# Evacuating the turned attention probabilities of the first batch straight from PSUM into their high and low halves

## The chip, the cores and the metric

The kernel runs on one core of one Trainium2 chip. The metric is device time in microseconds (us) for one launch; the lower the better. The core has five engines with instruction queues of their own: PE (TensorE, matrix products), DVE (VectorE), ACT (ScalarE), POOL (GpSimd) and SP (SyncE, which here only issues DMAs). SBUF is the on-chip memory of 128 partitions; PSUM is the accumulator memory of eight banks, into which PE writes.

## The reference

Cut to what matters, for `q`, `k`, `v` of shape (8 batches, 8 heads, 576 tokens, 64):

```python
k_p = k.reshape(B, H, Sp, 8, D).mean(axis=3)         # keys and values pooled by 8: Sp = 72
v_p = v.reshape(B, H, Sp, 8, D).mean(axis=3)
s = scale * q @ k_p^T
p = exp(s - max(s)); p = p / (sum(p) + 1e-9)
x = (p @ v_p), transposed to (4608 tokens, 512)
x = ((x @ w1) * (x @ w2)) @ w3 @ w_out               # 512 -> 1024 -> 1024 -> 512
h = x @ w_in                                         # 512 -> 2048
out = (h * sigmoid(1.702 * h)) @ w_out2              # 2048 -> 512
```

The weights arrive as 64-bit floats; the kernel turns them into 32-bit ones itself.

## The kernel before, in words

All large products are made at nearly the accuracy of 32-bit floats out of a faster format (called fp32r in the profile). Each operand is split into a high half (the value rounded to that format) and a low half (the value minus the high half), and a product is three matmuls: high by high, high by low, low by high (`mm3`, L114 to L116; `mm3u`, L709, in the last stage). A split is one copy on ACT (`split`, L104) and one subtraction on DVE or POOL (L105).

The work has three stages.

1. A first stage, some 130 us long. The weights `w_out`, `w3`, `w1`, `w2` are loaded and converted, tile by tile, by `Conv.step` (two activations on ACT, L166 and L168; a shift on DVE, L169; an addition on POOL, L172), then split. `w3` is also turned on PE (L508) and multiplied with `w_out` (`w3_mm`, which goes through `mm3` into two accumulators). Between these steps, `tick` calls `tick_first`, which takes the first batch's attention forward: four groups (n = 0 to 3, `NPE` = 4), each of two heads.
2. The products with `w1` and `w2` and the folded `w3 w_out`, block by block of 512 tokens, with the attention of the other seven batches (groups 4 to 31) between them, in the same `tick`.
3. The last expert layer, whose weights stream from DRAM.

The attention of a group goes through these functions: `g0` turns k and q (L255, L256) and sums k by eight; `g1` makes the scores on PE (L277) into two PSUM banks and subtracts the row maximum (L282, L284); `g2` is the exponential (L293); `g3` normalizes (L300 to L303); `g4` makes the turned probabilities and their halves; `g_va` and `g_vb` pool the values and split them into `vm` and `vt` (POOL, L324 to L342; ACT, L338 to L341); `g6` multiplies (L380 to L383) into the group's two banks and splits the result into the block's `x` (L390, L391). For groups 0 to 3 the turn is made on PE against an identity matrix; the others turn with DVE (L314).

In `g4` of a group n < 4 the two banks that held the scores take the transposes: the first bank four of 128 columns (L351), the second one of 64 (L354) and three of 32 partitions (L356), and, once the first bank is read out, the last two of 32 partitions go there (L360, L361). ACT copies them out to the SBUF tiles `p0` (128 partitions, L352, L358) and `p1` (32 partitions, L359, L362). Then come the halves: `ph` holds high and low of `p0`, by an ACT copy (L368) and a POOL subtraction (L369), each of 576 columns; `pt` holds high, high again and low of `p1` in partitions 0 to 31, 32 to 63 and 64 to 95, by two ACT copies (L370, L371) and a POOL subtraction (L372). All four tiles exist once each (one buffer), in every group. Even groups of the first four use the banks `wk[2:]`, odd ones `acc[2:]`. The profile calls `p0` and `p1` together `p`, and a few tiles by the name of the slot that they lie in (`s`).

The order in which an engine gets its instructions isn't just that of the program: the context is opened with `schedule_with_timeline_sim=True`, and a planner with costs of its own places each engine's instructions, keeping the dependences, among them that a tile with one buffer isn't written again before its readers of the last group are done. In the order of the program, `tick_first` runs `g6(n)` at tick 2n + 6, ahead of `g4(n + 1)` in the same tick:

```python
for n in range(NPE):
    if t == 2 * n + 6:
        g6(n)
...
    elif s == 4:          # s = t - 2 * n
        g4(n)
        g_va(n)
    elif s == 5:
        g_vb(n)
```

SP issues the loads of weights (L151), of k and q (L229, four transfers of 72 KB each) and of v (L249, L250) in one queue.

Of the kernel before, what the change touches and what calls it, by code (L numbers as in the profile page):

```python
# [8 lines left out]
F32R = mybir.dt.float32r  # L9
# [3 lines left out]
ALU = mybir.AluOpType  # L13
# [4 lines left out]
P = 128  # L18
T = 512
# [3 lines left out]
def pooled_attention_moe_moe2(  # L23
# [18 lines left out]
    nc = tc.nc  # L42
    B, H, S, D = q.shape
# [12 lines left out]
    NPE = HP  # L56
# [34 lines left out]
    def take_a(i, dtype=F32R):  # L91

        return slota_p.tile([P, 2, T], dtype, name=f"s{i}", tag=f"s{i}")
# [6 lines left out]
    def f32(ap):  # L100
        return ap.bitcast(F32)
# [22 lines left out]
    def sl(i, n=P):  # L124
        return slice(i * n, (i + 1) * n)
# [65 lines left out]
    with pa_ctx:  # L191
        pa = pa_ctx.enter_context(tc.tile_pool(name="pa", bufs=1))
# [6 lines left out]
            out=mask[:, 0], in_=mask[:, 0], compare_op=ALU.is_gt, fill=0.0,  # L199
            base=SK, pattern=[[0, D]], channel_multiplier=-1)  # L200
        nc.gpsimd.affine_select(
            out=mask[:, 1], in_=mask[:, 1], compare_op=ALU.is_ge, fill=0.0,
# [8 lines left out]
        for t in s_ts:  # L211
# [6 lines left out]
            out=ident, in_=ident, compare_op=ALU.is_equal, fill=0.0,  # L218
# [6 lines left out]
        g_q, g_k, g_v, g_s = {}, {}, {}, {}  # L225
# [38 lines left out]
        def banks_of(n):  # L264
            return acc[2:] if n < NPE and n % 2 else wk[2:]

        def s_of(n):
            return s_ts[n % 2 if n < NPE else 0]
# [26 lines left out]
        def g3(n):  # L295
            s_t = s_of(n)
            r = banks_of(n)[0][:, T - 2 * TT:]
            pv = s_t[:, :, :KW].rearrange("p t (a s) -> p t a s", s=SK)
            rv = r.rearrange("p (t a) -> p t a", a=2)
            nc.vector.tensor_reduce(out=rv, in_=pv, op=ALU.add, axis=AX.X)  # L300
            nc.vector.tensor_scalar_add(r, r, 1e-9)
            nc.vector.reciprocal(out=r, in_=r)
            nc.vector.tensor_tensor(  # L303
                out=pv, in0=rv.unsqueeze(3).to_broadcast([P, TT, 2, SK]), in1=pv, op=ALU.mult)
            p0 = pa.tile([P, TT, P], F32, name="p0", tag="p0")
            p1 = pa.tile([32, TT, P], F32, name="p1", tag="p1")
            g_s[n] = (p0, p1)
            if n < NPE:
                return
            for r in range(5):  # L310
                for c in range(4):
                    nt = TT if 32 * (c + 1) <= S - (TT - 1) * P else TT - 1
                    dst = p0[32 * r:32 * r + 32] if r < 4 else p1[:32]
                    nc.vector.transpose(  # L314
                        out=dst[:, :nt, 32 * c:32 * c + 32],
                        in_=s_t[32 * c:32 * c + 32, :nt, 32 * r:32 * r + 32])
# [26 lines left out]
                out=vt[32:64, D:], in0=vtf, in1=f32(vt[:32, D:]), op=ALU.subtract)  # L343

        def g4(n):
            p0, p1 = g_s.pop(n)
            if n < NPE:
                ps, s_t = banks_of(n), s_of(n)
                p0f, p1f = (t.rearrange("p t c -> p (t c)") for t in (p0, p1))
                for tt in range(4):  # L350
                    nc.tensor.transpose(ps[0][:, sl(tt)], s_t[:, tt, :P], ident)  # L351
                nc.scalar.copy(p0f[:, :T], ps[0])  # L352
                w = S - T
                nc.tensor.transpose(ps[1][:, :w], s_t[:w, 4, :P], ident[:w, :w])  # L354
                for tt in range(3):
                    nc.tensor.transpose(  # L356
                        ps[1][:32, w + tt * P:w + (tt + 1) * P], s_t[:, tt, P:], ident)
                nc.scalar.copy(p0f[:, T:S], ps[1][:, :w])  # L358
                nc.scalar.copy(p1f[:, :3 * P], ps[1][:32, w:w + 3 * P])  # L359
                nc.tensor.transpose(ps[0][:32, :P], s_t[:, 3, P:], ident)  # L360
                nc.tensor.transpose(ps[0][:32, P:P + w], s_t[:w, 4, P:], ident[:w, :w])  # L361
                nc.scalar.copy(p1f[:, 3 * P:S], ps[0][:32, :P + w])  # L362
            ph = pa.tile([P, 2, S], F32R, name="ph", tag="ph")
            pt = pa.tile([96, S], F32R, name="pt", tag="pt")
            g_s[n] = (ph, pt)
            s0 = p0.rearrange("p t c -> p (t c)")[:, :S]
            s1 = p1.rearrange("p t c -> p (t c)")[:, :S]
            nc.scalar.copy(ph[:, 0], s0)  # L368
            nc.gpsimd.tensor_tensor(out=ph[:, 1], in0=s0, in1=f32(ph[:, 0]), op=ALU.subtract)  # L369
            nc.scalar.copy(pt[:32], s1)  # L370
            nc.scalar.copy(pt[32:64], s1)  # L371
            nc.gpsimd.tensor_tensor(out=pt[64:96], in0=s1, in1=f32(pt[:32]), op=ALU.subtract)  # L372
# [32 lines left out]
        def tick_first():  # L405

            t = tick_n[0]
            tick_n[0] += 1
# [4 lines that stand above are left out]
                s = t - 2 * n  # L413
                if s == 0 and n == 0:
                    g0(0)
                elif s == 1:
                    g1(n)
                elif s == 2:
                    g2(n)
                    g0(n + 1)  # L420
                elif s == 3:
                    g3(n)
                elif s == 4:
# [4 lines that stand above are left out]
            if t == 2 * NPE + 4:  # L428
                tick_n[0] = 4 * NPE
                give(s_sl)  # L430

        def tick():
            t = tick_n[0]
            if t < 4 * NPE:
                return tick_first()
            tick_n[0] += 1
            n, s = divmod(t, 4)
            if s == 0:
                if NPE <= n - 1 < NG:
                    g4(n - 1)  # L440
            elif s == 1:
                if n < NG:
                    g1(n)
            elif s == 2:
                if NPE <= n - 1 < NG:
                    g6(n - 1)
                if n < NG:
                    g2(n)
                    g_va(n)
                if n + 1 < NG:  # L450
                    g0(n + 1)
            elif n < NG:
                g3(n)
                g_vb(n)
# [147 lines left out]
        for blk in range(NB):  # L602
            x = [x_slot(blk, c) for c in range(KM)]
            if blk == NB - 2:

                pa_ctx.close()
                pa = pa_ctx.enter_context(tc.tile_pool(name="pc", bufs=1, reuse_waits="tile"))
# [10 lines left out]
            for f in range(NF1):  # L618
# [6 lines left out]
                if blk == NB - 1:  # L625
                    give(w1_s.pop(f))
                    give(w2_s.pop(f))
                    if 0 <= f - FA < KM:

                        t = take_a(f - FA)  # L630
# [41 lines left out]
    with tc.tile_pool(name="pb", bufs=1, reuse_waits="tile") as pb, \  # L672
# [206 lines left out]
        for k, f in enumerate(FO):  # L879
            bk = bank()  # L880
            w = ready.pop(("h", 0, f))
# [29 lines left out]
        for pr in range(1, NPAIR + 1):  # L911
# [17 lines left out]
            for fp in range(NFP):  # L929
# [4 lines left out]
                for name, i in ORDER:  # L934
# [6 lines left out]
                    if name in PART:  # L941
                        s, h = PART[name]
                        w = ready[s, pr, 2 * fp + i][:, h]
                    else:
                        w = ready[name, pr, fp][:, i]
# [53 lines left out]
            src = {"M5": 0, "M7": 1, "M3": 2, "M2": 3, "M4": 3, "M6": 4}  # L999
# [12 lines left out]
            m1, U, V, n = [], [], [], 0  # L1012
# [116 lines left out]
```

## Time and profile before

| | us |
|---|---|
| median of 3 runs | 1477.42 |
| lowest and highest of them | 1476.0, 1481.82 |
| the profiled execution, its own time | 1479.71 |
| span of its profile | 1478.0 |
| PE busy in the span | 1438.7 |

The span is the time between the first and the last instruction in the profile; the profiled execution's own time holds 1.71 us around it. An engine's busy time counts its instructions alone. "Idle before" an instruction, in brackets at the end of a timeline row, is the time for which its engine did nothing ahead of it, and behind the arrow stands what ended that time.

### The profile page before, as it was taken

The page shows a single profiled execution, that of the slowest core. Times are in us where ns is not written, and L with a number is a line of the kernel's source. Part 1 is how long each engine was busy: PE and PEld are TensorE (multiplying, and loading weights), DVE is VectorE, ACT ScalarE, POOL GpSimd, SP SyncE. Part 2 cuts the span into 40 slices and gives each one's busy share as a digit, 9 for nine tenths or more (in the row PEclk, how much of TensorE's full clock was granted, in tenths as well). Part 3 has the DMA queues.
Part 4 walks back from the last instruction along what each step waited for, and adds up shares of the span by engine and source line. Part 5 has one row for each costly group of instructions (what it writes and reads, how often), then busy time and mean ns, then how long its engine had stood idle before and what let it go on. Part 6 is the DMA issues. An engine that isn't in the chain of part 4 may idle for free.

```text
span 1478.0 us, 19436 instructions
## 1 busy us (share of the span) xinstructions
PE 1438.7 (97%) x6536; PEld 1190.0 (81%) x6536; DVE 988.7 (67%) x1728; ACT 693.9 (47%) x1212; POOL 489.0 (33%) x589
## 2 busy tenths in 40 slices
PE   6979999999999999999999999999999999999998
PEld 4867888888888888888788887888788888888886
DVE  7888998878787877654737255683559354944554
ACT  7875444434343433366635344552455244534442
POOL 8789656554545555366733100000000000000000
PEclk9989999999999999999999999999999999999999
DMA  9992233323232311199879978877677766785665
GB/s 265 248 233 48 57 85 57 80 46 78 49 77 49 77 33 37 42 325 344 309 236 398 325 243 276 294 211 221 194 244 224 221 197 221 239 234 180 194 213 139
DMA packets 294436, 267.64 MB, mean 181 GB/s; under 512 B 201664, under 2 KB 226240, under 8 KB 294336
## 3 DMA queue, kind: packets, MB, share of 16 engines
q1 hardware_dynamic: 291648, 265.09, 59.8%
q10 hardware_dynamic: 2688, 1.31, 0.3%
q8 instruction: 52, 0.85, 0.2%
q14 instruction: 48, 0.39, 0.1%
HBM read 209.72 MB, written 56.62 MB: 180 GB/s over the span
## 4 chain that ended last, share of the span: by engine, by line
PE 82%; DMA 7%; DVE 5%; ACT 2%; SPq 2%; issue 1%; POOL 1%; DVEq 0%; ACTq 0%; POOLq 0%
PE bk L709 39%; PE wk L114 8%; PE wk L115 8%; PE wk L116 8%; PE acc L114 4%; PE acc L115 4%; PE acc L116 4%; PE wk L277 2%; DMA wud<-wt 2%; DVE p L314 1%; SPq L229 1%; DMA st<-wind 1%; PE bk L115 1%; PE bk L116 1%; PE bk L114 1%
## 5 line engine op out<-in xcount | busy, mean ns | idle before, releaser
L709 PE MATMUL bk<-mv,st 128*128 128x512 f32 x1152 | 272.6, 391 | 0.7 <-DMA st<-wud 0.7
L709 PE MATMUL bk<-xM,st 128*128 128x512 f32 x1092 | 259.0, 390 | 3.9 <-DMA st<-wind 3.7
L709 PEld LDWEIGHTS bk<-mv,st 128*128 128x128 f32 x1152 | 217.3, 189 | 46.3 <-issue 1.1
L709 PEld LDWEIGHTS bk<-xM,st 128*128 128x128 f32 x1092 | 204.5, 188 | 48.6 <-issue 2.5
L114 PE MATMUL wk<-s,s 128*128 128x512 f32 x576 | 227.0, 396 | 2.8 <-DVE a L641 1.2
L116 PE MATMUL wk<-s,s 128*128 128x512 f32 x576 | 224.9, 391 | 2.1 <-DVE s L105 2.1
L115 PE MATMUL wk<-s,s 128*128 128x512 f32 x576 | 224.9, 391 | 0.0
L314 DVE STREAM_TRANSPOSE p<-s_t 32x160 f32<-32x160 f32 (+1 forms) x560 | 178.5, 319 | 10.3
L114 PE MATMUL acc<-s,s 128*128 128x512 f32 x352 | 134.8, 406 | 8.2 <-ACT s L104 3.2
L115 PE MATMUL acc<-s,s 128*128 128x512 f32 x352 | 141.4, 402 | 0.9 <-POOL s L105 0.8
L116 PE MATMUL acc<-s,s 128*128 128x512 f32 x352 | 140.4, 399 | 0.0
L114 PEld LDWEIGHTS wk<-s,s 128*128 128x128 f32 x576 | 108.5, 189 | 26.2 <-DVE a L641 2.1
L116 PEld LDWEIGHTS wk<-s,s 128*128 128x128 f32 x576 | 108.3, 188 | 24.8 <-DVE s L105 2.3
L115 PEld LDWEIGHTS wk<-s,s 128*128 128x128 f32 x576 | 108.4, 188 | 22.1 <-DVE s L391 0.4
L105 DVE TENSOR_TENSOR mv<-g,mv 128x1024 fp32r<-128x1024 f32 x80 | 97.8, 1222 | 33.6 <-ACT mv L104 32.2
L104 ACT CAST mv<-g 128x1024 fp32r<-128x1024 f32 x80 | 84.3, 1054 | 71.8 <-PE bk L709 71.4
L172 POOL TENSOR_TENSOR cv<-cv,s 128x512 int32<-128x512 int32 x72 | 97.5, 1364 | 28.6 <-DVE cv L169 21.1
L105 POOL TENSOR_TENSOR s<-a,s 128x512 fp32r<-128x512 f32 x56 | 72.5, 1294 | 82.5 <-ACT s L104 62.7
L638 ACT COPY a<-wk 128x512 f32<-128x512 f32 x72 | 42.1, 585 | 110.5 <-PE wk L116 89.7
L369 POOL TENSOR_TENSOR ph<-p,ph 128x576 fp32r<-128x576 f32 x32 | 45.7, 1429 | 126.5 <-ACT ph L368 123.9
L114 PEld LDWEIGHTS acc<-s,s 128*128 128x128 f32 x352 | 67.8, 193 | 23.4 <-ACT s L104 5.2
L115 PEld LDWEIGHTS acc<-s,s 128*128 128x128 f32 x352 | 68.2, 194 | 15.0 <-POOL s L105 2.0
(190 smaller groups left out, 2357.9 us busy)
## 6 DMA issues: line engine op xcount, KB each, us to landing
st<-wud SPq DMA_DIRECT2D x96, 512.0 KB, 4.4
st<-wind SPq DMA_DIRECT2D x66, 512.0 KB, 4.7
st<-wind SPq DMA_DIRECT2D x76, 256.0 KB, 3.9
s<-in_moe_w_dram SPq DMA_DIRECT2D x32, 512.0 KB, 6.4
wind<-s SPq DMA_DIRECT2D x32, 512.0 KB, 5.4
s<-in_moe_w_out_dram SPq DMA_DIRECT2D x24, 512.0 KB, 6.5
kr<-in_k_dram SPq DMA_DIRECT2D x128, 72.0 KB, 2.6
qr<-in_q_dram SPq DMA_DIRECT2D x128, 72.0 KB, 2.6
```

The source lines that it names most:

```text
L104: nc.scalar.copy(dst[:, 0], src)
L105: lo_eng.tensor_tensor(out=dst[:, 1], in0=src, in1=f32(dst[:, 0]), op=ALU.subtract)
L114: nc.tensor.matmul(o, a[:, 0, a_sl], b[:, 0, b_sl], start=first, stop=False)
L115: nc.tensor.matmul(o, a[:, 0, a_sl], b[:, 1, b_sl], start=False, stop=False)
L116: nc.tensor.matmul(o, a[:, 1, a_sl], b[:, 0, b_sl], start=False, stop=last)
L172: nc.gpsimd.tensor_tensor(out=w.bitcast(I32), in0=w.bitcast(I32), in1=lo_w.bitcast(I32), op=ALU.add)
L229: nc.sync.dma_start(dst[32 * c:32 * c + 32], src[b, 2 * hp + c // 2, :, 32 * (c % 2):32 * (c % 2) + 32].rearrange("(g t) d -> t g d", t=32))
L277: nc.tensor.matmul(sc[half][:, i * KW:(i + 1) * KW], qT[:, sl(tt)], mov, start=True, stop=True)
L314: nc.vector.transpose(out=dst[:, :nt, 32 * c:32 * c + 32], in_=s_t[32 * c:32 * c + 32, :nt, 32 * r:32 * r + 32])
L369: nc.gpsimd.tensor_tensor(out=ph[:, 1], in0=s0, in1=f32(ph[:, 0]), op=ALU.subtract)
L638: nc.scalar.copy(a, pa_)
L709: nc.tensor.matmul(o, w[:, x, m], b[:, y], start=first and n == 0, stop=last and n == 2, skip_group_check=True)
```

## The change

For groups 0 to 3, `g4` no longer copies the transposes to `p0` and `p1`. ACT copies each piece of a bank straight to the high half in `ph` (512 and 64 columns) or `pt` (384 and 192 columns), DVE subtracts that from the same piece in PSUM to give the low half, and for `pt` ACT copies the piece from PSUM a second time, to the second high half. POOL has no part in it any more. `ph` and `pt` are taken at the head of `g4`; `p0` and `p1` are no longer taken in `g3` for these groups. Groups 4 to 31 are as before.

```diff
@@ g3 @@
+            if n < NPE:
+                return
             p0 = pa.tile([P, TT, P], F32, name="p0", tag="p0")
             p1 = pa.tile([32, TT, P], F32, name="p1", tag="p1")
             g_s[n] = (p0, p1)
-            if n < NPE:
-                return
@@ g4 @@
-            p0, p1 = g_s.pop(n)
+            ph = pa.tile([P, 2, S], F32R, name="ph", tag="ph")
+            pt = pa.tile([96, S], F32R, name="pt", tag="pt")
             if n < NPE:
                 ps, s_t = banks_of(n), s_of(n)
-                p0f, p1f = (t.rearrange("p t c -> p (t c)") for t in (p0, p1))
+                w = S - T
+
+                def main(c, src):
+                    nc.scalar.copy(ph[:, 0, c], src)
+                    nc.vector.tensor_tensor(
+                        out=ph[:, 1, c], in0=src, in1=f32(ph[:, 0, c]), op=ALU.subtract)
+
+                def tail(c, src):
+                    nc.scalar.copy(pt[:32, c], src)
+                    nc.vector.tensor_tensor(
+                        out=pt[64:96, c], in0=src, in1=f32(pt[:32, c]), op=ALU.subtract)
+                    nc.scalar.copy(pt[32:64, c], src)
+
                 for tt in range(4):
                     nc.tensor.transpose(ps[0][:, sl(tt)], s_t[:, tt, :P], ident)
-                nc.scalar.copy(p0f[:, :T], ps[0])
-                w = S - T
+                main(slice(0, T), ps[0])
                 nc.tensor.transpose(ps[1][:, :w], s_t[:w, 4, :P], ident[:w, :w])
                 for tt in range(3):
                     nc.tensor.transpose(
                         ps[1][:32, w + tt * P:w + (tt + 1) * P], s_t[:, tt, P:], ident)
-                nc.scalar.copy(p0f[:, T:S], ps[1][:, :w])
-                nc.scalar.copy(p1f[:, :3 * P], ps[1][:32, w:w + 3 * P])
+                main(slice(T, S), ps[1][:, :w])
+                tail(slice(0, 3 * P), ps[1][:32, w:w + 3 * P])
                 nc.tensor.transpose(ps[0][:32, :P], s_t[:, 3, P:], ident)
                 nc.tensor.transpose(ps[0][:32, P:P + w], s_t[:w, 4, P:], ident[:w, :w])
-                nc.scalar.copy(p1f[:, 3 * P:S], ps[0][:32, :P + w])
-            ph = pa.tile([P, 2, S], F32R, name="ph", tag="ph")
-            pt = pa.tile([96, S], F32R, name="pt", tag="pt")
+                tail(slice(3 * P, S), ps[0][:32, :P + w])
+                g_s[n] = (ph, pt)
+                return
+            p0, p1 = g_s.pop(n)
             g_s[n] = (ph, pt)
```

## Rows read from the trace of the kernel before

**Rows 1.** Windows of the whole span: us, busy us of each engine, PE clock, DMA share, GB/s

```profile
0.00:130.00 130.00, 104.86 (x475) 81.50 (x476) 107.12 (x175) 100.91 (x207) 106.00 (x121) 0.93 0.87 218
250.00:640.00 390.00, 390.00 (x1873) 329.80 (x1872) 304.12 (x736) 158.01 (x353) 200.10 (x276) 1.00 0.28 66
700.00:1478.00 778.00, 765.04 (x3354) 629.30 (x3352) 441.37 (x520) 348.28 (x475) 64.27 (x48) 1.00 0.74 239
```

**Rows 2.** Windows of ten us, from group 1's `g4` to group 4's turn

```profile
60.00:70.00 10.00, 10.00 (x53) 7.85 (x52) 7.66 (x16) 9.84 (x25) 5.94 (x7) 1.00 0.91 218
70.00:80.00 10.00, 7.05 (x44) 5.49 (x41) 6.85 (x12) 7.37 (x17) 6.93 (x9) 1.00 1.01 224
80.00:90.00 10.00, 8.53 (x34) 6.98 (x35) 8.92 (x15) 8.28 (x19) 9.69 (x12) 0.83 1.07 212
90.00:100.00 10.00, 8.64 (x35) 6.53 (x34) 6.46 (x10) 8.32 (x18) 7.94 (x10) 0.83 0.98 231
100.00:110.00 10.00, 7.54 (x37) 5.84 (x36) 9.83 (x12) 6.86 (x16) 9.40 (x12) 0.93 1.19 249
110.00:120.00 10.00, 9.72 (x44) 7.95 (x43) 9.92 (x22) 7.52 (x15) 9.63 (x10) 0.90 0.36 67
```

**Rows 3.** Timeline of PE: start, us, what [idle before <-releaser]

```profile
75.70 0.40 PE L380 MATMUL acc<-ph,vm 128*128 128x288 f32 x1 [0.61 <-DVE s L284]
81.47 0.76 PE L114 MATMUL acc<-s,s 128*128 128x512 f32 x1 [2.84 <-ACT ph L368]
94.02 0.50 PE L114 MATMUL acc<-s,s 128*128 128x512 f32 x1 [1.36 <-DVE s L105]
104.73 0.54 PE L382 MATMUL acc<-ph,vm 128*128 128x288 f32 x2 [0.39 <-POOL vm L339]
107.79 0.50 PE L116 MATMUL wk<-s,s 128*128 128x512 f32 x1 [2.06 <-DVE s L105]
```

**Rows 4.** Tiles `ph`, `pt`, `p`, first 112 us: count, ns shortest/median/longest, first and last start

```profile
L368 ACT CAST ph<-p x4: 655/668/677, 36.9 to 93.3; 128x576 fp32r<-128x576 f32 x4
L369 POOL TENSOR_TENSOR ph<-p,ph x4: 1412/1429/1612, 38.4 to 95.5; 128x576 fp32r<-128x576 f32 x4
L370 ACT CAST pt<-p x4: 655/660/667, 40.7 to 94.6; 32x576 fp32r<-32x576 f32 x4
L372 POOL TENSOR_TENSOR pt<-p,pt x4: 1420/1429/1487, 41.8 to 99.1; 32x576 fp32r<-32x576 f32 x4
L359 ACT COPY p<-wk x2: 463/464/466, 36.5 to 70.9; 32x384 f32<-32x384 f32 x2
L362 ACT COPY p<-wk x2: 293/302/311, 38.7 to 75.8; 32x192 f32<-32x192 f32 x2
```

**Rows 5.** Line 105 on DVE from PSUM, first 130 us

```profile
L105 DVE TENSOR_TENSOR s<-wk,s x16: 675/690/692, 10.7 to 85.7; 128x512 fp32r<-128x512 f32 x16
```

**Rows 6.** Timeline of DVE, a subtraction of 64 columns

```profile
65.17 0.21 DVE L391 TENSOR_TENSOR s<-wk,s 128x64 fp32r<-128x64 f32 x1
```

**Rows 7.** Line 169 on DVE, first 130 us

```profile
L169 DVE TENSOR_SCALAR cv<-cv x39: 385/911/3137, 5.3 to 129.2; 128x512 uint32<-128x512 uint32 x39
```

**Rows 8.** Timelines of DVE (first row) and POOL around group 3

```profile
101.82 3.14 DVE L169 TENSOR_SCALAR cv<-cv 128x512 uint32<-128x512 uint32 x1
99.12 1.43 POOL L372 TENSOR_TENSOR pt<-p,pt 32x576 fp32r<-32x576 f32 x1
102.98 1.28 POOL L105 TENSOR_TENSOR s<-cv,s 128x512 fp32r<-128x512 f32 x1
104.23 0.45 POOL L339 TENSOR_TENSOR vm<-vf,vm 128x128 fp32r<-128x128 f32 x1
```

**Rows 9.** Timeline of ACT around group 2's `g4`, and line 390 later

```profile
68.56 0.59 ACT L352 COPY p<-wk 128x512 f32<-128x512 f32 x1
80.79 0.68 ACT L368 CAST ph<-p 128x576 fp32r<-128x576 f32 x1
111.55 0.21 ACT L390 CAST s<-acc 128x64 fp32r<-128x64 f32 x1 [0.19 <-DVE s L391]
```

## The prediction

> **What bounds the kernel now.** I read the windows of the whole span first, because the change touches four groups of a kernel with 32. The reader should compare PE's busy time with the length of each window. From 250 to 640 us PE is busy all of 390.00 us, from 700 to the end 765.04 of 778 [rows 1]. There the kernel is bound by PE, and nothing that ACT, DVE or POOL gain would show. In the first 130 us PE is busy 104.86 us only, at a granted clock of 0.93, while DVE, ACT and POOL are each busy 101 to 107 us and the DMA share is 0.87 [rows 1]. So this stage is bound by no single engine: four of them and the loads hand on to each other. A microsecond that PE gains in it comes out at the end, since PE is full afterwards; one that PE doesn't see is worth nothing.
>
> The change acts from group 0's `g4` (its first copy to `ph` starts at 36.9 us [rows 4]) to group 3's product. The windows of ten us show where PE has anything to win: it is full from 60 to 70, and from 70 to 120 it is idle 2.95, 1.47, 1.36, 2.46 and 0.28 us, 8.5 in all [rows 2]. The clock means of 0.83, 0.83, 0.93 and 0.90 in the four windows from 80 on cost another 1.7 + 1.7 + 0.7 + 1.0 = 5.1 us of full-speed work [rows 2]. Together 13.6 us is the most that the stretch can give back. That estimate ends at 120 us, where the change no longer acts.
>
> Then the timeline of PE, for what ended each idle time. The largest were ended by VectorE's splits or by what stands beside them: 2.84 us at 81.47, 1.36 at 94.02, 2.06 at 107.79; one of 0.39 at 104.73 by POOL's low half of the values [rows 3]. None of the five waits for a low half of `ph` or `pt`. What the change takes away is thus not itself on PE's path, and can help only through the queues that it stood in.
>
> **What goes.** POOL loses two subtractions per group, 1.43 us each [rows 4]: 2.86 us, 11.4 us in four groups. ACT loses three copies of 576 columns at 0.66 to 0.67 us, 2.00 us together, of which two rows stand [rows 4].
>
> **What comes.** ACT gets the two short copies to `pt` a second time, 0.464 + 0.302 us [rows 4]. Its four copies out of PSUM stay and only change their target. Net, ACT loses 2.00 - 0.77 = 1.23 us per group, 4.9 in all. DVE gets four subtractions per group with one side in PSUM. The one of 512 columns costs 0.69 us [rows 5], the one of 64 0.21 [rows 6]; on the line between these two, 0.55 for 384 and 0.35 for 192 columns (ACT's copies of 32 partitions take the time that their columns call for, so I don't expect fewer partitions to be cheaper or dearer). That is 1.80 us per group, 7.2 in all. PE's transposes and products stay as they are, and no DMA is added or removed.
>
> **Where it lies on the path.** First, POOL. Group 3's subtraction to `pt` ends at 100.55, and POOL then has a backlog: line 105 at 102.98 and the values' low half at 104.23 [rows 8]. PE waits 0.39 us for the latter [rows 3]. With 2.86 us of work gone ahead of it, this wait goes: 0.39 us. In the same place VectorE's shift (L169) takes 3.14 us [rows 8], where the shortest takes 0.385 and the median 0.911 [rows 7]; it began at 101.82 and ended with POOL's run of work. The VectorE split behind it is what PE waits 2.06 us for at 107.79 [rows 3]. If the shift is held by one POOL instruction of 1.28 us [rows 8] in place of several, it ends 3.14 - 1.28 = 1.86 us earlier. I take 1.86 (bounds: nothing, if other POOL work slides into the same place, and 2.75, if the shift takes 0.385).
>
> The page "SBUF — State Buffer" of the Trainium skill (section "Who interferes with whom") says that VectorE, in some instructions, and GpSimd lock a shared port pair for a whole instruction. By that rule up to 11.4 us of VectorE waiting could go with POOL's 11.4 us, instead of the 1.86 taken here; the shift of 3.14 us agrees with the rule, but the sum goes by the row.
>
> Of the clock's loss after these gaps, 0.7 us from 100 to 110 and 1.0 from 110 to 120 [rows 2], I count half as regained, 0.85 us (bounds nothing and 1.7). ACT was busy 9.84 of 10 us from 60 to 70 [rows 2], so 1.23 us less there may let the loads behind it start sooner. Against this stand waits of ACT, below, 3 x 0.19 = 0.57 us per group; of the 0.66 us that is left I count half, 0.33, because the DMA share is at 0.91 to 1.19 up to 110 us [rows 2] and an earlier issue finds busy DMA engines. Gains: 0.39 + 1.86 + 0.85 + 0.33 = 3.4 us.
>
> **The waits that come.** ACT's copies and VectorE's subtractions now read the same PSUM bank in turn. In the trace line 390's copy of 64 columns waits 0.19 us for VectorE's subtraction of other columns in the same bank [rows 9]. So three copies per group (`pt`'s first in the second bank and the second high half twice) wait for VectorE, and everything queued on ACT behind them waits too: conversions (L166, L168) and splits (L104). Price: 0.19 us each by that row, up to 3.14 us when a shift is stuck ahead [rows 8].
>
> The page "PSUM — Partial Sum Buffer" (section "PSUM bank collisions raise a hardware error") of the Trainium skill has this as a rule: two engines may not access the same bank and quadrant at one time, reads included. The row of 0.19 us shows the wait that keeps to it.
>
> VectorE's added 1.80 us mostly finds room: it is idle 2.3, 3.2, 1.1 and 3.5 us in the windows from 60 to 100 [rows 2]. The exception is group 3. Its three short subtractions, 1.11 us, fall just before the split that PE waits for at 94.02 [rows 3]. I count half, 0.6 us (bounds 0 and 1.1).
>
> Third, `ph` has one buffer. Until now the first copy of group 2 went to `p0` at 68.56, and only the copy to `ph` at 80.79 had to let group 1's product read the old halves [rows 9]; that product began at 75.70 [rows 3]. Now the first copy has to wait for it, until about 77.0 (eight matmuls), 8.4 us later than before. PE's last two transposes need that bank read out by ACT and then VectorE, 0.59 + 0.69 us more: 78.3. PE is in order, and what is queued behind them waits. Before, PE sat idle 2.84 us up to 81.47 anyway [rows 3], which hides the wait if the planner puts the transposes there; put right behind the product they hold PE for 1.3 us. I take 0.7.
>
> **Sum.** 3.4 - 0.6 - 0.7 = 2.1 us less. The profiled execution's own 1479.71 us (span 1478.0 and 1.71 around it) would become 1477.6. It lay 2.3 us above the median, 1477.42; off the median the forecast is 1475.3. Half a per cent, about what a measurement of this kernel can tell from no change, is 7.4 us: below 1470.0 is faster, above 1484.8 slower.
>
> **Rivals.**
> *The loads bound the stretch.* Then ACT's and POOL's relief ends in waiting for weights and keys: 1477.4. For it: the DMA share near 1 up to 110 us [rows 2]. Against: the waits of PE at 94.02 and 107.79 were ended by VectorE, not a load [rows 3].
> *POOL's relief cascades.* If VectorE's shifts are held less all along, two thirds of the 13.6 us come back: 9.0 us, 1468.4. For it: the shift's median of 0.911 against 0.385 [rows 7], over 39 shifts 20 us. Against: POOL's own 106 us [rows 1] fall only by a ninth.
> *ACT waits for VectorE, and the time grows.* Twelve copies wait in one bank for a subtraction that itself may stand behind a held shift. At 0.19 + 0.911 = 1.10 us each that is 13.2 us, less the 4.9 saved: 8.3 us, and 1485.7 if all of it reaches PE. It decides from (7.4 + 4.9) / 12 = 1.0 us per wait. For it: ACT is full from 60 to 70. Against: it has 2.6, 1.7 and 1.7 us idle in the next three windows [rows 2], and the planner may put other work ahead of a copy that waits.
>
> **Chances and range.** Forecast 0.50, loads 0.28, cascade 0.12, ACT's waits 0.10. The planner may also change the order on every engine, which the rows can't price; it widens each case by about 3 us. Faster by over 0.5%: the cascade and a tail of the forecast, 0.14. Slower: ACT's waits, 0.10. Within: 0.76. The range of 1468 to 1484 leaves out about half of the cascade, most of ACT's waits and a little of the rest, 2 in 10 together.
>
> **What the profile after would show.** No subtraction to `ph` or `pt` on POOL before 110 us; four more on DVE per group at 0.69, 0.55, 0.35 and 0.21 us, hardly varying; a shorter shift near 101; the gap at 107.79 gone; group 2's first copy behind group 1's product. PE's busy time after 130 us should not change. The prediction is wrong if ACT's idle time before lines of `g4` grows to several us and PE's idle with it, or if PE's gaps from 70 to 120 nearly vanish.

## The result, and the profile after

The changed kernel takes 1486.44 us in the median of six runs (1484.08 to 1490.33), the kernel before, run beside it, 1479.12 us (1476.0 to 1481.82). The ratio is 1.0051, with a 95% interval of 1.0035 to 1.0066: about 7.5 us slower. The forecast was 1475.3 us in a range of 1468 to 1484, so the time lies outside the range and on the other side of no change. The profiled execution has a span of 1484.2 us.

First the engines' sums over the span, from the pages of the two kernels (before, then after):

```profile
PE 1438.7 (97%) x6536; PEld 1190.0 (81%) x6536; DVE 988.7 (67%) x1728; ACT 693.9 (47%) x1212; POOL 489.0 (33%) x589
```

```profile
PE 1439.6 (97%) x6536; PEld 1190.6 (80%) x6536; DVE 989.6 (67%) x1744; ACT 691.0 (47%) x1208; POOL 477.6 (32%) x581
```

POOL has lost 11.4 us, as worked out; ACT 2.9 (of 4.9 worked out) and VectorE has gained 0.9 only (of 7.2). PE does the same work in the same time. So POOL and VectorE did what was forecast or better, ACT was relieved of less than forecast, and the time still grew. The windows of the whole span (the columns of [rows 1]) show where:

```profile
0.00:130.00 130.00, 99.64 (x446) 76.14 (x447) 103.78 (x189) 94.86 (x199) 93.49 (x117) 0.92 0.88 224
250.00:640.00 390.00, 390.00 (x1877) 329.94 (x1876) 303.70 (x742) 150.60 (x340) 195.54 (x271) 1.00 0.26 58
700.00:1484.00 784.00, 772.34 (x3395) 635.94 (x3393) 445.44 (x525) 355.60 (x487) 70.84 (x53) 1.00 0.75 241
```

From 250 to 640 us nothing has changed: PE is full. From 700 us on PE is idle for 11.7 us, where it was 13.0. In the first 130 us PE is busy 99.64 us, where it was 104.86 [rows 1], with every other engine less busy too. The second block's last copy to `x2o` marks the end of the first stage's effect. The tile's rows give its first and last start in the first 340 us, before and after:

```profile
L597 ACT COPY x2o<-acc x4: 567/585/589, 187.9 to 274.4; 128x512 f32<-128x512 f32 x4
```

```profile
L610 ACT COPY x2o<-acc x4: 581/586/588, 199.4 to 282.7; 128x512 f32<-128x512 f32 x4
```

274.4 has become 282.7 us: 8.3 us later, and the rest of the span is 2.1 us shorter. PE's count of matmuls (behind its busy time) by 640 us says the same, before and after:

```profile
0.00:640.00 640.00, 613.62 (x2919) 511.01 (x2920) 515.61 (x1163) 308.57 (x673) 386.45 (x512) 0.99 0.41 96
```

```profile
0.00:640.00 640.00, 607.25 (x2878) 505.04 (x2879) 510.61 (x1171) 295.74 (x652) 368.50 (x498) 0.98 0.39 92
```

41 matmuls are missing; at the 1873 in 390.00 us of [rows 1] that is 8.5 us. In these two traces the whole loss stands in the first stage. There the windows of ten us that answer to [rows 2] read:

```profile
70.00:80.00 10.00, 7.27 (x40) 5.30 (x39) 7.47 (x14) 6.65 (x14) 7.06 (x7) 0.90 1.08 250
80.00:90.00 10.00, 9.77 (x34) 7.28 (x34) 6.22 (x12) 7.74 (x19) 6.94 (x11) 0.76 0.94 188
90.00:100.00 10.00, 5.78 (x27) 4.37 (x27) 8.64 (x19) 6.36 (x16) 7.84 (x10) 0.83 1.10 235
100.00:110.00 10.00, 4.45 (x17) 3.64 (x18) 7.97 (x17) 6.34 (x17) 4.98 (x10) 0.76 0.77 158
110.00:120.00 10.00, 8.97 (x40) 7.17 (x40) 7.46 (x23) 6.16 (x14) 8.48 (x13) 0.90 0.76 195
```

PE's idle time from 70 to 120 us is now 2.73 + 0.23 + 4.22 + 5.55 + 1.03 = 13.8 us (8.5 before), and its clock's loss 1.0 + 2.4 + 1.7 + 2.4 + 1.0 = 8.5 us (5.1 before). PE's timeline shows what ended the idle time, as [rows 3] did:

```profile
77.31 0.40 PE L393 MATMUL acc<-ph,vm 128*128 128x288 f32 x1 [2.28 <-DVE s L284]
91.08 0.40 PE L393 MATMUL wk<-ph,vm 128*128 128x288 f32 x1 [1.31 <-ACT pt L361]
94.88 0.50 PE L393 MATMUL wk<-ph,vm 128*128 128x288 f32 x1 [3.14 <-ACT pt L361]
104.26 0.40 PE L393 MATMUL acc<-ph,vm 128*128 128x288 f32 x1 [3.42 <-ACT pt L361]
107.06 0.61 PE L393 MATMUL acc<-ph,vm 128*128 128x288 f32 x1 [2.13 <-ACT pt L361]
```

The last four rows, those of groups 2 and 3, were ended by ACT's second high half (L361). The product's first matmul (L393) doesn't read `pt`. What it shares with L361 is the PSUM bank: L361 is now the bank's last reader, and the matmul overwrites it. The tile's rows say the same from both sides (the first two rows: what ended the idle time before instructions on `pt`; the last two: who waited for L361; totals in us, times):

```profile
  DVE ph L354: 0.6, 1
  DVE pt L359: 0.2, 1
  PE acc L393: 5.5, 2
  PE wk L393: 4.5, 2
```

PE waited 10.0 us for it. ACT itself waited 0.8 us for VectorE, in all of `pt`. How the last read came so late is seen in group 3, on ACT (five rows) and VectorE (the last):

```profile
98.16 0.70 ACT L353 CAST ph<-acc 128x512 fp32r<-128x512 f32 x2
99.64 0.47 ACT L358 CAST pt<-acc 32x384 fp32r<-32x384 f32 x1 [0.60 <-DVE ph L354]
102.15 0.65 ACT L168 ACTIVATE s<-s 128x512 int32<-128x512 uint32 x1 [2.04 <-DMA s<-in_moe_w_dram]
103.74 0.47 ACT L361 CAST pt<-acc 32x384 fp32r<-32x384 f32 x1
106.70 0.31 ACT L361 CAST pt<-acc 32x192 fp32r<-32x192 f32 x1
105.12 0.35 DVE L359 TENSOR_TENSOR pt<-acc,pt 32x192 fp32r<-32x192 f32 x1
```

The first copy out of the bank starts at 98.16, the last read ends at 107.01. That is 8.9 us. Between them stand two turns of ACT and VectorE, each behind what the planner's lists put ahead of it. ACT's list wasn't full of work: ACT stood idle for 2.04 us before a conversion (L168) whose weights had not been loaded, and the second copies came behind it. Before, group 3's first and last copy out of its banks, and the first matmul of its product, were these:

```profile
88.28 0.59 ACT L352 COPY p<-acc 128x512 f32<-128x512 f32 x1 [0.48 <-POOL vm L339]
92.28 0.30 ACT L362 COPY p<-acc 32x192 f32<-32x192 f32 x1
103.08 0.39 PE L380 MATMUL acc<-ph,vm 128*128 128x288 f32 x1
```

That is 88.28 to 92.58, 4.3 us, and the product came 10.5 us later.

The longer hold is only a part of it: the copies also start later, in group 3 by 9.9 us. In group 2 the hold has hardly grown (86.34 to 94.83, 8.5 us; before, 68.56 [rows 9] to 76.1 [rows 4], 7.5 us), but the first copy starts 17.8 us later. The rows around it, in the changed kernel:

```profile
72.62 0.50 PE L368 MATMUL wk<-ident,s_t 128*32 128x128 f32 x3
85.89 0.29 PE L395 MATMUL acc<-ph,vm 128*128 128x288 f32 x1
86.34 0.69 ACT L353 CAST ph<-wk 128x512 fp32r<-128x512 f32 x2
86.96 0.82 DVE L354 TENSOR_TENSOR ph<-wk,ph 128x512 fp32r<-128x512 f32 x2 [3.47 <-ACT ph L353]
```

Group 2's first eight transposes were done at 73.1 us. But `ph` has one buffer, and the last matmul that reads group 1's halves in it stands at 85.89 in PE's new order, where group 1's whole product had been over at 77.0. ACT's copy comes right behind it, and VectorE has been idle for 3.47 us.

The durations themselves are as worked out from [rows 4 to 6]; here three rows of the even groups:

```profile
L354 DVE TENSOR_TENSOR ph<-wk,ph x4: 204/432/692, 38.2 to 87.6; 128x512 fp32r<-128x512 f32 x2, 128x64 fp32r<-128x64 f32 x2
L359 DVE TENSOR_TENSOR pt<-wk,pt x4: 349/448/551, 41.3 to 93.3; 32x384 fp32r<-32x384 f32 x2, 32x192 fp32r<-32x192 f32 x2
L361 ACT CAST pt<-wk x4: 308/389/470, 44.4 to 94.5; 32x384 fp32r<-32x384 f32 x2, 32x192 fp32r<-32x192 f32 x2
```

VectorE's shift (L169), the row that answers to [rows 7]:

```profile
L169 DVE TENSOR_SCALAR cv<-cv x39: 378/442/4395, 5.1 to 147.7; 128x512 uint32<-128x512 uint32 x39
```

Its median has fallen from 0.911 to 0.442 us; the longest one is longer. The fall can't be put down to POOL's relief: under the five neutral edits with the planner on, told below, the kernel before has medians of 0.53 to 0.62 us with all of POOL's work kept.

### The profile page after: what moved, and what is told of

Same layout as the page of the kernel before. It is cut to its first block, busy times and chain, and to the rows that moved or that the text cites. A ratio compares the mean times of both kernels' runs of the same rounds, so it can differ in the third digit from the quotient of the medians.

```text
span 1484.2 us, 19430 instructions
## 1 busy us (share of the span) xinstructions
PE 1439.6 (97%) x6536; PEld 1190.6 (80%) x6536; DVE 989.6 (67%) x1744; ACT 691.0 (47%) x1208; POOL 477.6 (32%) x581
## 4 chain that ended last, share of the span: by engine, by line
PE 84%; DMA 4%; DVE 3%; POOL 1%; issue 1%; ACT 0%; SPq 0%; ACTq 0%; POOLq 0%; DVEq 0%
PE bk L722 40%; PE wk L114 8%; PE wk L115 8%; PE wk L116 8%; PE acc L115 4%; PE acc L116 4%; PE acc L114 4%; PE wk L277 2%; DMA st<-wind 1%; DMA wud<-wt 1%; PE bk L114 1%; PE bk L115 1%; PE bk L116 1%; POOL cv L172 1%; DVE cv L169 1%
## 5 line engine op out<-in xcount | busy, mean ns | idle before, releaser
L105 DVE TENSOR_TENSOR mv<-g,mv 128x1024 fp32r<-128x1024 f32 x80 | 97.8, 1222 | 33.3 <-ACT mv L104 31.9
L105 POOL TENSOR_TENSOR s<-a,s 128x512 fp32r<-128x512 f32 x56 | 72.4, 1293 | 97.3 <-ACT s L104 72.1
L382 POOL TENSOR_TENSOR ph<-p,ph 128x576 fp32r<-128x576 f32 x28 | 40.4, 1442 | 124.0 <-ACT ph L381 124.0
```

The lines of the kernel that those rows point to most:

```text
L105: lo_eng.tensor_tensor(out=dst[:, 1], in0=src, in1=f32(dst[:, 0]), op=ALU.subtract)
```

## The experiments

Two theories had to be told apart, with others beside them. **Data theory:** the changed copies cost the time, by holding the banks longer and by hand-overs. **Order theory:** the planner makes other lists for all engines when anything changes (in the traces, 282 of PE's 6536 matmuls don't fit into one common order of the two kernels, and group 3's product begins with PE's 356th matmul instead of the 380th), and the kernel before happens to have good ones. All ratios are against the kernel before, run on the same chip, with 95% intervals.

### Parts of the change

**Second high half from SBUF** (to the changed kernel):

```diff
-                    nc.scalar.copy(pt[32:64, c], src)
+                    nc.scalar.copy(pt[32:64, c], f32(pt[:32, c]))
```

> The changed kernel, but ACT takes the second high half of pt from the first one in SBUF, no longer from PSUM. Bank theory (the products of groups 2 and 3 wait 10.0 us because ACT's second copy is the last reader of their banks): the banks come free after VectorE's subtraction, those waits fall to 5 us or less and no product waits for the second copy in its first matmul; 1.000 to 1.003 of before. Order theory (the planner has placed the products too close behind the transposes, whatever reads the banks): the products wait as long, now for VectorE, 1.004 to 1.006. VectorE theory (its added 7.2 us are the loss): 1.005, as the changed kernel.

1.0014 (1.0000 to 1.0027), as the bank theory had it; the order theory's forecast failed here. PE's rows for the first matmuls of groups 2 and 3 in this kernel:

```profile
90.81 0.30 PE L393 MATMUL wk<-ph,vm 128*128 128x288 f32 x1
92.77 0.40 PE L393 MATMUL wk<-ph,vm 128*128 128x288 f32 x1 [0.33 <-DVE pt L359]
100.21 0.40 PE L393 MATMUL acc<-ph,vm 128*128 128x288 f32 x1 [1.17 <-ACT vm L338]
100.58 0.30 PE L393 MATMUL acc<-ph,vm 128*128 128x288 f32 x1
```

The 10.0 us of waiting have become 1.5, none of it for the second copy, and the last `x2o` copy starts at 275.6 us. Group 3's product begins with PE's 352nd matmul, as early as in the changed kernel. But this edit too made another list: 229 matmuls don't fit into one order with the changed kernel's, nearly as many as the change itself moved. So the waits went with the read, but that the time did is not shown.

**Second high half by POOL, from SBUF** (to the changed kernel):

```diff
-                    nc.scalar.copy(pt[32:64, c], src)
+                    nc.gpsimd.tensor_copy(pt[32:64, c], pt[:32, c])
```

> The changed kernel with the second high half copied by POOL from SBUF, so that ACT has one copy per piece and each bank is free after VectorE's subtraction. Bank theory: as the run with ACT's second copy from SBUF or better, 0.998 to 1.002. Order theory: another draw of lists, 0.999 to 1.007.

1.0020 (1.0005 to 1.0034): the same again, by another way and with other lists. The products of groups 2 and 3 waited 1.0 us for a bank's last reader.

**Both ACT copies first** (to the changed kernel):

```diff
                     nc.scalar.copy(pt[:32, c], src)
+                    nc.scalar.copy(pt[32:64, c], src)
                     nc.vector.tensor_tensor(
                         out=pt[64:96, c], in0=src, in1=f32(pt[:32, c]), op=ALU.subtract)
-                    nc.scalar.copy(pt[32:64, c], src)
```

> The changed kernel with both ACT copies of each tail piece made one after the other, and VectorE's subtraction behind them, so that the bank goes from engine to engine once less; all from PSUM. Bank theory in its form of alternation (each hand-over through two full queues costs): the waits fall by about half, 1.001 to 1.004. Order theory: group 3's first products stand at the same place in PE's list as in the changed kernel, 1.004 to 1.006. VectorE theory: 1.005.

1.0040 (1.0026 to 1.0053): within what two theories allowed. The trace tells more than the time. All reads still come from PSUM, only with one turn between the engines less, and the products of groups 2 and 3 waited 1.6 us for a bank's last reader instead of 10.0. By 640 us PE has run as many matmuls as with the second high half from SBUF (that run first, then this one), 24 to 26 more than in the changed kernel:

```profile
0.00:640.00 640.00, 611.82 (x2902) 509.05 (x2903) 514.08 (x1178) 301.29 (x661) 370.03 (x501) 0.98 0.40 95
```

```profile
0.00:640.00 640.00, 607.44 (x2904) 505.10 (x2905) 515.00 (x1178) 301.93 (x662) 370.32 (x501) 0.99 0.40 95
```

So the late last read hangs on the order ACT, VectorE, ACT as much as on the second read from PSUM. Why the medians of the two still differ by 0.26% the traces don't show (spans of 1482.7 and 1483.5 us).

**The tail as before** (`ph` changed, `pt` through `p1` and POOL):

```diff
-                    nc.scalar.copy(pt[:32, c], src)
-                    nc.vector.tensor_tensor(
-                        out=pt[64:96, c], in0=src, in1=f32(pt[:32, c]), op=ALU.subtract)
-                    nc.scalar.copy(pt[32:64, c], src)
+                    nc.scalar.copy(p1f[:, c], src)
...
+                nc.scalar.copy(pt[:32], s1)
+                nc.scalar.copy(pt[32:64], s1)
+                nc.gpsimd.tensor_tensor(out=pt[64:96], in0=s1, in1=f32(pt[:32]), op=ALU.subtract)
```

> The changed kernel with the part of 32 partitions (pt) made as before, through p1 with two ACT copies and POOL's subtraction; the part of 128 partitions (ph) stays changed. Bank theory: the chain of ACT, VectorE and ACT again on the tail is gone, no long wait of the products; 0.999 to 1.002. Order theory: this kernel's list for PE has group 3's products some 24 rows later than the changed one, so 0.999 to 1.002 too. VectorE theory: half its added work is left, 1.002 to 1.003. Single-buffer theory (ph can't be written before the last group's product): 1.004 to 1.005, since ph is as changed.

1.0058 (1.0040 to 1.0077). Here the bank theory failed: no second copy reads PSUM, and nothing is won. The longest waits of PE in the first stage (who waited <- for whom: total, times, longest):

```profile
PE acc L396 <- ACT vm L339: 5.0, 1, 5.0
PE wk L114 <- DVE a L657: 3.8, 2, 2.8
PE wk L524 <- POOL cv L172: 3.6, 3, 1.4
PE acc L371 <- DVE ph L356: 3.1, 1, 3.1
PE acc L396 <- DVE s L284: 2.5, 1, 2.5
```

PE now stands at group 3's product for the values' high half, and at one of group 3's transposes until VectorE has read `ph`'s bank (the wait that the prediction had priced at 0 to 1.3 us).

**The main part as before** (`pt` changed, `ph` through `p0` and POOL):

```diff
-                    nc.scalar.copy(ph[:, 0, c], src)
-                    nc.vector.tensor_tensor(
-                        out=ph[:, 1, c], in0=src, in1=f32(ph[:, 0, c]), op=ALU.subtract)
+                    nc.scalar.copy(p0f[:, c], src)
...
+                nc.scalar.copy(ph[:, 0], s0)
+                nc.gpsimd.tensor_tensor(out=ph[:, 1], in0=s0, in1=f32(ph[:, 0]), op=ALU.subtract)
```

> The reverse: ph made as before, through p0 with POOL's subtraction; pt stays changed. Bank theory: the tail still alternates between ACT and VectorE in both banks and ACT's second copy is still the last reader, so the products wait several us for it; 1.003 to 1.006. Order theory: its list for PE has group 3's products 23 rows later than the changed kernel's, group 2's at the same place; half the waits go, 1.000 to 1.003. VectorE theory: 1.002 to 1.003. Single-buffer theory: 0.999 to 1.001.

1.0072 (1.0057 to 1.0087), above every forecast. The bank theory failed in its waits too: PE waited 0.3 us for the second copy, not several. Each half of the change loses as much as the whole, or more. No sum of costs of the two parts gives that, so it speaks against VectorE's added work. It doesn't settle the single buffer: here `pt` is still written straight from the banks into its one buffer, and with the tail as before `ph` is, so in both a group's copies out of the banks have to wait for the last group's product. Two buffers were not tried.

**Before, with the two subtractions on VectorE, from SBUF:**

```diff
-            nc.gpsimd.tensor_tensor(out=ph[:, 1], in0=s0, in1=f32(ph[:, 0]), op=ALU.subtract)
+            lo = nc.vector if n < NPE else nc.gpsimd
+            lo.tensor_tensor(out=ph[:, 1], in0=s0, in1=f32(ph[:, 0]), op=ALU.subtract)
...
-            nc.gpsimd.tensor_tensor(out=pt[64:96], in0=s1, in1=f32(pt[:32]), op=ALU.subtract)
+            lo.tensor_tensor(out=pt[64:96], in0=s1, in1=f32(pt[:32]), op=ALU.subtract)
```

> The kernel before with p0 and p1 kept, and only the two POOL subtractions of groups 0 to 3 made by VectorE, from SBUF: POOL's relief without PSUM held longer and without hand-overs in a bank. Data theory: no new reader of a bank, POOL relieved by 11.4 us, 0.997 to 1.001. Order theory: its lists move as far from those of before as the changed kernel's do, 1.000 to 1.007, more likely slower.

0.9997 (0.9980 to 1.0014). POOL's relief, with VectorE's added work beside it, is worth nothing that can be measured; the interval leaves room for a gain of 3 us. 226 of PE's matmuls don't fit into one order with the kernel before's, so another list needn't cost.

### The same edit in both kernels

If the copies cost the time, any neutral edit made in both kernels leaves the changed one slower by the same. These edits change lists, not work.

**q's load ahead of k's**, in every group:

```diff
-            g_k[n] = ...; load_blocks(g_k[n], k, b, hp)
             g_q[n] = ...; load_blocks(g_q[n], q, b, hp)
+            g_k[n] = ...; load_blocks(g_k[n], k, b, hp)
```

In the kernel before: 

> The kernel before with q's load issued ahead of k's in every group: no instruction more or less, but the planner then makes other lists for all engines (about 1360 of PE's rows move). Order theory: a chance change of the lists alone moves the time as much as the change did, so 0.3 per cent or more to one side, more likely slower, 1.002 to 1.007. Data theory: 0.999 to 1.002.

In the changed kernel: 

> The changed kernel with q's load ahead of k's, which makes other lists once more (about 1340 of PE's rows move). Order theory: another draw, anywhere from 0.999 to 1.007, and not reliably above the kernel before with the same swap, which took 1.0052. Data theory: both losses add, 1.008 to 1.012.

**Group 3's products six ticks later:**

```diff
-                if t == 2 * n + 6:
+                if t == 2 * n + 6 and n < NPE - 1:
                     g6(n)
...
-                if NPE <= n - 1 < NG:
+                if NPE - 1 <= n - 1 < NG:
                     g6(n - 1)
```

In the kernel before: 

> The kernel before with group 3's products six ticks later in the program, the control for the same edit of the changed kernel (1.0058). Order theory: again slower than before without any added read, 1.001 to 1.007. Data theory: 0.999 to 1.002, so that the changed kernel's 1.0058 is its own.

In the changed kernel: 

> The changed kernel with group 3's products (g6) put six ticks later in the program, behind group 4's scores. Theory that PE's list has the products too close behind the transposes: group 3's waits of 5.5 us for ACT's second copy go, 1.001 to 1.003. Theory that the time of ACT and VectorE is lost, wherever PE waits for it: PE waits elsewhere, 1.004 to 1.006.

**The planner's timeline off:**

```diff
-    with _tile.TileContext(nc, schedule_with_timeline_sim=True) as tc:
+    with _tile.TileContext(nc) as tc:
```

In the kernel before: 

> The kernel before with the planner's timeline switched off, so that the engines' lists keep nearer to the order of the program; the reference for the next run. No theory depends on its time against before; it may be 0 to 3 per cent slower.

In the changed kernel: 

> The changed kernel with the planner's timeline switched off in the same way. The two lists for SP are then the same, and those for PE differ in some 70 of 3849 rows, while with the planner on some 1300 rows differ. Data theory (banks held by more reads, ACT and VectorE in turn): the loss stays, this is 0.3 to 0.7 per cent slower than the run before it in this call. Order theory (the planner's new lists are the loss, not the copies themselves): the two agree within 0.2 per cent, or this one is a little faster by POOL's relief.

**w2's tiles ahead of w1's:**

```diff
+            conv.add(col_tile(w2, f), None, conv.to(w2_s, f, nc.vector))
             conv.add(col_tile(w1, f), None,
                      conv.to(w1_s, f, a=f - FA if 0 <= f - FA < NA else None))
-            conv.add(col_tile(w2, f), None, conv.to(w2_s, f, nc.vector))
```

In the kernel before: 

> The kernel before with each tile of w2 loaded and converted ahead of that of w1. Order theory: a new draw of lists, 1.000 to 1.007. Data theory: 0.999 to 1.002. It is one half of a pair with the next run.

In the changed kernel: 

> The changed kernel with the same edit. Data theory: 0.3 to 0.6 per cent slower than the run before it. Order theory: within 0.3 per cent of it, to either side.

**Attention one conversion later:**

```diff
-            if i >= 4 and tick_n[0] < 20:
+            if i >= 5 and tick_n[0] < 20:
```

In the kernel before: 

> The kernel before with the first batch's attention started one conversion later. Order theory: a new draw, 1.000 to 1.008. Data theory: 0.999 to 1.002. One half of a pair with the next run.

In the changed kernel: 

> The changed kernel with the same edit. Data theory: 0.3 to 0.6 per cent slower than the run before it. Order theory: within 0.3 per cent of it, to either side.

**VectorE and POOL swapped for w_out's low halves:**

```diff
-                 conv.to(wo_s, j, nc.gpsimd if i % 2 else nc.vector, j,
+                 conv.to(wo_s, j, nc.vector if i % 2 else nc.gpsimd, j,
```

In the kernel before: 

> The kernel before with VectorE and POOL swapped for the low halves of w_out's eight tiles (they alternate). Order theory: a new draw of lists, 1.000 to 1.008. Data theory: 0.999 to 1.002. One half of a pair with the next run.

In the changed kernel: 

> The changed kernel with the same edit. Data theory: 0.3 to 0.6 per cent slower than the run before it. Order theory: within 0.3 per cent of it, to either side.

| edit in both | before with it, to before | changed with it, to before | changed to before, both with it |
|---|---|---|---|
| none | 1 | 1.0051 (1.0035 to 1.0066) | +0.51% |
| q first | 1.0052 (1.0033 to 1.0070) | 1.0035 (1.0021 to 1.0049) | -0.17% |
| group 3 later | 1.0062 (1.0042 to 1.0082) | 1.0058 (1.0040 to 1.0077) | -0.04% |
| timeline off | 1.0556 (1.0532 to 1.0579) | 1.0527 (1.0504 to 1.0549) | -0.27% |
| w2 first | 1.0039 (1.0025 to 1.0053) | 1.0057 (1.0038 to 1.0075) | +0.18% |
| attention later | 1.0004 (0.9991 to 1.0018) | 1.0025 (1.0011 to 1.0040) | +0.21% |
| w_out swapped | 1.0118 (1.0099 to 1.0136) | 1.0070 (1.0049 to 1.0091) | -0.47% |

The last column is the quotient of the two ratios. Over the six edits its mean is -0.09%, and its sign goes both ways. The data theory's 0.3 to 0.7% came in none of them; the order theory's forecast for the last three pairs (within 0.3%) failed once, for `w_out` swapped, where the changed kernel is 0.47% faster. The halves of the first two pairs ran on different chips, those of the other four on one; all are compared through the kernel before on their own chip. With intervals of 0.13 to 0.24% to either side of each ratio, a quotient is good to some 0.2 to 0.3%, and six that scatter like these leave room for a mean of some 0.2% to the slower side.

With the timeline off, 31 of PE's matmuls don't fit into one order of the two kernels, and SP's order is the same. There the medians are 1562.38 us (1560.82 to 1564.90) for before and 1558.33 us (1557.71 to 1559.59) for the changed kernel, which is 4.0 us faster. In this order no product waits for the second copy. So the pair shows that the copies by themselves cost nothing there, not that a wait for a bank would cost nothing.

What a neutral edit does to the kernel before is seen in PE's waits of the first stage (view as for the tail above). With q first:

```profile
PE acc L114 <- ACT s L104: 6.4, 3, 3.5
PE acc L114 <- DVE s L105: 3.0, 1, 3.0
PE wk L114 <- ACT s L104: 2.8, 1, 2.8
PE wk L114 <- DVE a L641: 2.4, 1, 2.4
```

The kernel has no second copy from PSUM, and PE loses as much at other instructions: the last `x2o` copy starts at 282.3 us, 7.9 us later than in the kernel before. With `w_out` swapped it is 291.3 us. The same edit in the changed kernel, 282.6 us, has the waits for the second copy again:

```profile
PE wk L393 <- ACT pt L361: 3.8, 2, 2.3
PE wk L277 <- DVE s L404: 3.7, 1, 3.7
PE acc L393 <- ACT pt L361: 3.6, 1, 3.6
PE acc L114 <- ACT s L104: 3.0, 2, 2.4
```

So it is under all five edits with the planner on: the products wait 3.3 to 7.4 us for the second copy (10.0 without an edit), and the changed kernel is still, on average, no slower than the kernel before with the same edit, whose waits stand elsewhere. A wait that a trace shows is not the loss by that alone.

## Why the prediction was wrong

**What bounds the kernel, and what stays full:** right. In the two traces the loss is all in the first stage, and PE is full from 250 to 640 us.

**What goes and what comes:** right in size for POOL and for the new subtractions. POOL lost the 11.4 us worked out, and the new subtractions took 0.69, 0.55, 0.35 and 0.20 to 0.22 us. VectorE's busy time grew by 0.9 us instead of 7.2: its 40 shifts took 32.6 us in all instead of 37.2, and twelve splits from SBUF (L105) 13.8 instead of 16.0. ACT's busy time fell by 2.9 us where 4.9 had been worked out.

**"Where it lies on the path", the gains of 3.4 us:** wrong as a sum. It took two gaps of the old timeline and shortened them one by one, with half of the clock's loss behind them and a part of ACT's relief. The gaps at 104.73 and 107.79 are gone as such, and so is VectorE's shift of 3.14 us at 101.82, but gaps of 3.42 and 2.13 us now stand at 104.26 and 107.06. POOL's relief was real, but no gain from it was measured (0.9997, with room for 3 us). The prediction also misread its largest gap: the 2.84 us at 81.47 [rows 3] were ended by ACT's copy L368, one of the three that the change takes away, so by that row something of it did stand on PE's path.

**"The waits that come":** this step failed first. It followed the hand-overs in a bank to ACT, at 0.19 us each, and VectorE's read of the first bank to PE's transposes, at 0.7 us. It did not follow the bank to its next writer, a term that it put at nothing without a reason. The product of `g6` writes the same banks; it used to find them read out by ACT's four copies long before, because `p0` and `p1` took the data off PSUM, and now waits for the second high half. That was 10.0 us on PE, where the prediction had 0.6 + 0.7 us for all waits that come. The wait for the single buffer it did see, and mis-sized: group 2's first copy came behind group 1's product, as it said, but 17.8 us later than before, not 8.4, because the new order had moved that product's second half back; so the reads of the bank ended late too. With this read out of PSUM the waits went, and 0.37% of the 0.51% (ACT) or 0.31% (POOL) came back; both runs have other lists as well.

**"The planner may also change the order ... by about 3 us":** this term was too small, and it decides the result. Five edits that change no work, made in the kernel before with the planner on, cost between 0.04 and 1.18% (0.6 to 17.5 us); the lowest is no loss that can be measured, the other four are 0.39% or more. The unedited kernel before lies at the fast end of the six orders of it that were run. The changed kernel's lists spread from 1.0025 to 1.0070, its 1.0051 in the middle.

Together: the loss of 0.51% is not a fixed price of the changed copies, since under the same edit in both kernels it is gone on average, and with nearly the same lists on PE the changed kernel wins 0.27%. In the list that the planner made for it, PE's longest waits are for the late last read of the banks; that they are what makes the 0.51% is not shown. That the new read and the new lists are linked (the planner reckoned on an earlier end of the chain than the chip gave) fits the rows, but was not shown: no run kept the list of before and changed the copies alone with the planner on.

**The rivals:** "ACT waits for VectorE" gave 1485.7 us, near the measured time, but by luck, for its reason did not hold: ACT waited 0.8 us, where 13.2 were priced. The wait took place on PE. No cascade came of POOL's relief, and none of PE's gaps shown was ended by a load, though one load held ACT for 2.04 us on the way to group 3's last read.

**What remains open** is why each half of the change alone (1.0058 and 1.0072) costs as much as both. Their waits stand at other instructions than those of the whole, which fits other lists, but two draws of a list settle nothing. The single buffer, which every version of the change keeps in one of the two tiles or both, is a rival that no run took away.

No version beat the kernel before. The nearest are the subtractions on VectorE from SBUF (0.9997) and the second high half from SBUF (1.0014).

## What to carry to other kernels

When a copy out of PSUM is replaced by several reads of it, follow the bank to whoever writes it next, not only to the readers, and the tile that is now written from it to its last reader: a copy to SBUF that looks superfluous may be what lets PE have the bank early (in group 3 it was held 4.3 us with the copy and 8.9 without) and lets a group's copies start before the last group's product is done. Where a planner makes the engines' lists, a stage in which four engines hand on to each other can move by a per cent when nothing but an order changes; make the same neutral edit in both kernels a few times before a change of half a per cent is credited or blamed. A gap in a trace that is shortened by relief on a third engine is a gain only if the next wait behind it is known.

## What the runs showed of the hardware

VectorE's shift of 128x512 words, with the same operands, took from 0.378 to 4.395 us in the first 150 us of the changed kernel. In the two traces the shifts beside which POOL did nothing took 0.39 to 0.43 us; the longest ones, 4.395 us at 130.63 in the changed kernel and 3.14 us at 101.82 before [rows 8], had POOL at work all along, though a few others with POOL at work all along took no more than 0.43. The page "SBUF — State Buffer" of the Trainium skill (section "Who interferes with whom") says that VectorE's scalar operations in their two-port modes and GpSimd's instructions lock each other out for a whole instruction. The long shifts agree with that, except that they lasted over several of POOL's instructions, of 0.4 to 1.3 us each. The fall of the median doesn't bear on it, as other orders of the kernel before show it too.
